# Start-up and last store of a one-core SiLU MLP forward and backward kernel: dummy matmuls, order and size of the first loads, buffers of the first transposes, and a split last group

## Chip, cores, metric

The kernel runs on one core of a Trainium2 chip. The metric is the device time of one execution in microseconds (us); lower is better. "Span" is the time from the first to the last instruction in a trace, which is about 2 us shorter than the device time. A run of a kernel is a set of executions; I quote medians and, where two kinds of execution appear, each kind. PE is the matmul engine (TensorE), DVE the vector engine, ACT the scalar engine, SP the engine that only issues transfers here.

## The reference

```python
B, S, D, F = 1, 2048, 640, 1536          # all bfloat16
def _fwd_reference(x, w1, w2):
    h = jnp.einsum("bsd,df->bsf", x, w1)
    h = silu(h)
    return jnp.einsum("bsf,fd->bsd", h, w2)
# results: out, and the gradients of x, w1, w2 for a given grad_out (jax.vjp)
```

## The kernel before

Work is cut into four chunks of 512 rows. Stage P of a chunk computes h = w1ᵀ·xᵀ and ga = w2·gᵀ for 12 tiles of F, five 512-wide matmuls each, and from them the activation and its gradient. Stage O multiplies back for out and the gradient of x. At the end come the two weight gradients, gw2 and gw1. The first chunk needs xᵀ, gᵀ and w2ᵀ, which PE makes by transposes into PSUM tiles (`tp` in the traces); DVE (0.49 us for 640 columns) or ACT (0.69 us) copies them to SBUF tiles (`xT_c`, `gT_c`, `w2T_sb`), from which PE's matmuls take them.

```python
    xn = gh_sb[:, NS - TPC : NS, 0:D]
    gn = a_sb[:, NS - TPC : NS, 0:D]
    nc.sync.dma_start(out=xn, in_=x2[0:SC, :]...)        # x, 640 KB, SP's queue
    nc.scalar.dma_start(out=gn, in_=g2[0:SC, :]...)      # grad_out, 640 KB, ACT's queue
    for fc in range(NFC):                                # three pieces of 512 columns or 4 row tiles
        nc.sync.dma_start(out=w1_sb[:, :, fc*FC:(fc+1)*FC], ...)       # 640 KB
        nc.scalar.dma_start(out=w2_sb[:, fc*FPC:(fc+1)*FPC, :], ...)   # 640 KB
    nc.sync.dma_start_transpose(out=w1T_sb[:], in_=w1[:, :])

    for t in range(TPC):                                 # 4 tiles of 128 rows
        tp = psO.tile([P, 16, P], bf16, tag="o")         # two buffers in all
        for i, src in enumerate((xn, gn)):
            for dk in range(ND):
                nc.tensor.transpose(tp[:, i*8 + dk, :], src[:, t, dk*P:(dk+1)*P], ident[:])
        nc.vector.tensor_copy(out=xT_c[...], in_=tp[:, 0:ND, :])
        nc.scalar.copy(out=gT_c[...], in_=tp[:, 8:8+ND, :])

    def w2T_transposes(fc): ...    # 20 transposes for 4 tiles; DVE copies 2048 wide, ACT 512 wide
    # ... stages P, T, O of four chunks, then gw2: not touched by the change
    groups = [(dt_, fc) for dt_ in range(ND) for fc in range(NFC)]     # gw1: 15 groups of 16 matmuls
    # ... pairs of groups; each is copied by ACT or DVE and stored; the 15th stands alone
```

Of the kernel before, what the change touches and what calls it, by code (L numbers as in the profile page):

```python
# [8 lines left out]
ACT = mybir.ActivationFunctionType  # L9
ALU = mybir.AluOpType  # L10
# [3 lines left out]
def kernel(  # L14
# [11 lines left out]
    nc = tc.nc  # L26
    P = 128
    bf16 = mybir.dt.bfloat16
    f32 = mybir.dt.float32
# [5 lines left out]
    NS, ND, NF = S // P, D // P, F // P  # L35
    FC = 512
    NFC = F // FC
    FPC = FC // P
    DH = D // 2
    SC = 512  # L40
    TPC = SC // P
    NCH = S // SC

    x2 = x.rearrange("b s d -> (b s) d")
    g2 = grad_out.rearrange("b s d -> (b s) d")
    o2 = out_0.rearrange("b s d -> (b s) d")
    gx2 = out_1.rearrange("b s d -> (b s) d")
    gw1 = out_2
# [4 lines left out]
    gh_sb = big.tile([P, NS, F], bf16)  # L53

    wO = ctx.enter_context(tc.tile_pool(name="wO", bufs=1))
    w2_sb = wO.tile([P, NF, D], bf16)
    w1T_sb = wO.tile([P, NF, D], bf16)
    ident = wO.tile([P, P], bf16)
# [6 lines left out]
    tmp = ctx.enter_context(tc.tile_pool(name="tmp", bufs=2))  # L65
    stage = ctx.enter_context(tc.tile_pool(name="stage", bufs=8))

    psO = ctx.enter_context(tc.tile_pool(name="psO", bufs=2, space=PSUM))
# [3 lines left out]
    psA = p1.enter_context(tc.tile_pool(name="psA", bufs=2, space=PSUM))  # L72

    w1_sb = early.tile([P, ND, F], bf16)
    w2T_sb = early.tile([P, ND, F], bf16)
    xT_c = early.tile([P, ND, SC], bf16)
    gT_c = early.tile([P, ND, SC], bf16)

    xn = gh_sb[:, NS - TPC : NS, 0:D]
    gn = a_sb[:, NS - TPC : NS, 0:D]  # L80
    nc.sync.dma_start(out=xn, in_=x2[0:SC, :].rearrange("(t p) d -> p t d", p=P))
    nc.scalar.dma_start(out=gn, in_=g2[0:SC, :].rearrange("(t p) d -> p t d", p=P))
    w1v = w1.rearrange("(k p) f -> p k f", p=P)
    w2v = w2.rearrange("(k p) d -> p k d", p=P)
    for fc in range(NFC):
        nc.sync.dma_start(
            out=w1_sb[:, :, fc * FC : (fc + 1) * FC], in_=w1v[:, :, fc * FC : (fc + 1) * FC]
        )
        nc.scalar.dma_start(
            out=w2_sb[:, fc * FPC : (fc + 1) * FPC, :], in_=w2v[:, fc * FPC : (fc + 1) * FPC, :]  # L90
        )
    nc.sync.dma_start_transpose(out=w1T_sb[:], in_=w1[:, :])

    for t in range(TPC):
        tp = psO.tile([P, 16, P], bf16, tag="o")
        for i, src in enumerate((xn, gn)):
            for dk in range(ND):
                nc.tensor.transpose(  # L98
                    tp[:, i * 8 + dk, :], src[:, t, dk * P : (dk + 1) * P], ident[:]
                )  # L100
        nc.vector.tensor_copy(out=xT_c[:, :, t * P : (t + 1) * P], in_=tp[:, 0:ND, :])  # L101
        nc.scalar.copy(out=gT_c[:, :, t * P : (t + 1) * P], in_=tp[:, 8 : 8 + ND, :])

    def w2T_transposes(fc):
        for dk0 in range(0, ND, 4):
            ndk = min(4, ND - dk0)
            tp = psO.tile([P, 16, P], bf16, tag="o")
            for i in range(ndk):
                for j in range(FPC):
                    ft = fc * FPC + j  # L110
                    nc.tensor.transpose(  # L111
                        tp[:, i * FPC + j, :],
                        w2_sb[:, ft, (dk0 + i) * P : (dk0 + i + 1) * P],
                        ident[:],
                    )
            src = tp[:, 0 : ndk * FPC, :].rearrange("p (i j) f -> p i (j f)", i=ndk)
            dst = w2T_sb[:, dk0 : dk0 + ndk, fc * FC : (fc + 1) * FC]
            if dk0 == 0:
                nc.vector.tensor_copy(out=dst, in_=src)  # L119
            else:  # L120
                nc.scalar.copy(out=dst, in_=src)

    def stage_P(c):
        for ft in range(NF):
            if c == 0 and ft % FPC == 0:
                w2T_transposes(ft // FPC)
            fsl = slice(ft * P, (ft + 1) * P)
            h_ps = psA.tile([P, SC], f32, tag="h")
            for dk in range(ND):
                nc.tensor.matmul(  # L130
                    h_ps[:], lhsT=w1_sb[:, dk, fsl], rhs=xT_c[:, dk, :],
                    start=(dk == 0), stop=(dk == ND - 1),
                )
            ga_ps = psA.tile([P, SC], f32, tag="ga")
            for dk in range(ND):
                nc.tensor.matmul(  # L136
                    ga_ps[:], lhsT=w2T_sb[:, dk, fsl], rhs=gT_c[:, dk, :],
                    start=(dk == 0), stop=(dk == ND - 1),
                )
            h3 = h_ps[:].rearrange("p (t s) -> p t s", t=TPC)  # L140
            ga3 = ga_ps[:].rearrange("p (t s) -> p t s", t=TPC)
            nc.scalar.activation(aT_c[:, :, ft, :], h3, ACT.Silu)  # L142
            nc.scalar.activation(h_ps[:], h_ps[:], ACT.Tanh, scale=0.5)  # L143
            omth = tmp.tile([P, TPC, P], f32, tag="omth")
            nc.scalar.activation(omth[:], h3, ACT.Identity, scale=-1.0, bias=1.0)  # L145
            nc.vector.scalar_tensor_tensor(  # L146
                out=omth[:], in0=aT_c[:, :, ft, :], scalar=-1.0, in1=omth[:],
                op0=ALU.add, op1=ALU.mult,
            )
            nc.vector.scalar_tensor_tensor(  # L150
                out=ghT_c[:, :, ft, :], in0=omth[:], scalar=2.0, in1=ga3,
                op0=ALU.add, op1=ALU.mult,
            )

    def stage_T(c):
        if c + 1 < NCH:
            nc.sync.dma_start_transpose(out=xT_c[:], in_=x2[(c + 1) * SC : (c + 2) * SC, :])
            nc.sync.dma_start_transpose(out=gT_c[:], in_=g2[(c + 1) * SC : (c + 2) * SC, :])
        for src, dst in ((aT_c, a_sb), (ghT_c, gh_sb)):
            nc.sync.dma_start_transpose(  # L160
                out=dst[:, c * TPC : (c + 1) * TPC, :].rearrange("p t (j r) -> p (t j) r", r=P),
                in_=src[:].rearrange("p t j s -> p (t j s)"),
            )
# [18 lines left out]

    for c in range(NCH):
        stage_P(c)
        if c == NCH - 1:
            p1.close()
            late = ctx.enter_context(tc.tile_pool(name="late", bufs=1))
            g_sb = late.tile([P, NS, D], bf16)
            x_sb = late.tile([P, NS, D], bf16)
            nc.sync.dma_start(out=g_sb[:], in_=g2.rearrange("(t p) d -> p t d", p=P))  # L190
            psW = ctx.enter_context(tc.tile_pool(name="psW", bufs=2, space=PSUM))
        stage_T(c)
        stage_O(c)
    nc.sync.dma_start(out=x_sb[:], in_=x2.rearrange("(t p) d -> p t d", p=P))

    for ft in range(NF):
        w_ps = psW.tile([P, 2, 512], f32, tag="w")
        for hf in range(2):
            for st in range(NS):
                nc.tensor.matmul(  # L200
                    w_ps[:, hf, :DH], lhsT=a_sb[:, st, ft * P : (ft + 1) * P],
                    rhs=g_sb[:, st, hf * DH : (hf + 1) * DH],
                    start=(st == 0), stop=(st == NS - 1),
                )
        w_sb = stage.tile([P, 2, DH], bf16, tag="o_sb")
        if ft % 2 == 0:
            nc.scalar.copy(out=w_sb[:], in_=w_ps[:, :, :DH])  # L207
        else:
            nc.vector.tensor_copy(out=w_sb[:], in_=w_ps[:, :, :DH])  # L209
        nc.sync.dma_start(  # L210
            out=gw2[ft * P : (ft + 1) * P, :], in_=w_sb[:].rearrange("p h d -> p (h d)")
        )
    groups = [(dt_, fc) for dt_ in range(ND) for fc in range(NFC)]
    for gi in range(0, len(groups), 2):
        pair = groups[gi : gi + 2]
        w_ps = psW.tile([P, 2, 512], f32, tag="w")
        for j, (dt_, fc) in enumerate(pair):
            for st in range(NS):
                nc.tensor.matmul(  # L219
                    w_ps[:, j, :], lhsT=x_sb[:, st, dt_ * P : (dt_ + 1) * P],  # L220
                    rhs=gh_sb[:, st, fc * FC : (fc + 1) * FC],
                    start=(st == 0), stop=(st == NS - 1),
                )
        for j, (dt_, fc) in enumerate(pair):
            w_sb = stage.tile([P, FC], bf16, tag="o_sb")
            if (gi + j) % 2 == 0:
                nc.scalar.activation(w_sb[:], w_ps[:, j, :], ACT.Copy, scale=0.5)  # L227
            else:
                nc.vector.tensor_scalar(  # L229
                    out=w_sb[:], in0=w_ps[:, j, :], scalar1=0.5, scalar2=None, op0=ALU.mult  # L230
                )
            nc.sync.dma_start(
                out=gw1[dt_ * P : (dt_ + 1) * P, fc * FC : (fc + 1) * FC], in_=w_sb[:]
            )


# [28 lines left out]
```

## Time and profile before

The median was 333.83 us (333.68 to 334.45, 5 executions). The profiled execution was a slowish one: 334.76 us, span 332.9 us.

Lines of the page of the kernel before: the span, PE's busy tenths in 40 slices of the span, and the shares by engine of the chain of work that ended last.

```profile
span 332.9 us, 4604 instructions
...
PE   1899999999999999999999999999999999999995
...
PE 92%; ACT 3%; DMA 2%; DVE 2%; issue 0%; ACTq 0%; DVEq 0%
```

PE is the bound, and only the two ends of the span have room. The waits of PE over the whole span (who waited for whom: us in total, times, longest) say how little there is in between.

```profile
PE tp L98 <- DMA gh_sb<-in_x_dram: 6.6, 1, 6.6
PE ga_ps L136 <- DVE w2T_sb L119: 0.6, 2, 0.3
PE h_ps L130 <- DVE xT_c L101: 0.6, 1, 0.6
PE tp L98 <- ACT gT_c L102: 0.2, 1, 0.2
```

PE waits 6.6 us for x, then little. But a busy PE need not be a fast one. The timeline of PE at the start (start us, duration us, engine, line, operation, names, count, idle time before) shows how fast it went.

```profile
6.63 0.71 PE L98 MATMUL tp<-ident,gh_sb 128*128 128x128 bf16 x5 [6.63 <-DMA gh_sb<-in_x_dram]
7.54 0.71 PE L98 MATMUL tp<-ident,a_sb 128*128 128x128 bf16 x5 [0.20 <-DMA a_sb<-in_grad_out_dram]
8.05 0.74 PE L98 MATMUL tp<-ident,gh_sb 128*128 128x128 bf16 x5
8.59 0.74 PE L98 MATMUL tp<-ident,a_sb 128*128 128x128 bf16 x5
9.56 0.69 PE L98 MATMUL tp<-ident,gh_sb 128*128 128x128 bf16 x5 [0.24 <-ACT gT_c L102]
...
12.44 0.59 PE L130 MATMUL h_ps<-xT_c,w_sb 128*128 128x512 bf16 x1 [0.58 <-DVE xT_c L101]
```

Five transposes start every 0.51 to 0.54 us, 107 ns apart. Of the twenty w2 transposes a little later, the first three (12.82, 12.93 and 13.03 us) are still 107 ns apart, and the rest 56 ns, by the start of each in the trace. PE ran at half rate until about 13.06 us, 6.4 us after the first of the transposes. Where the spacing halves like this I say below that the clock rose. (The profile's granted clock reads 1.00 through all of this, as its record in the trace begins only at 13.06 us. The spacing of the matmuls is what to read there.)

The transfers that PE needs first (names, queue, KB, median us from issue to landing):

```profile
w_sb<-in_w_dram ACTq DMA_DIRECT2D x3, 640.0 KB, 12.3
w_sb<-in_w_dram SPq DMA_DIRECT2D x3, 640.0 KB, 13.2
...
a_sb<-in_grad_out_dram ACTq DMA_DIRECT2D x1, 640.0 KB, 6.8
gh_sb<-in_x_dram SPq DMA_DIRECT2D x1, 640.0 KB, 5.8
```

And the end of the chain (start us, us, what): the last matmul ends at 329.41 us, the copy out of PSUM at 330.08, and 2.8 us more pass with the store and the end of the program.

```profile
321.03 8.38 PE w_ps L219 x38
...
329.48 0.60 ACT w_sb L227
```

### The profile page before, as it was taken

Reading aid. Unit: us, or ns where it says so; the run is one execution under the profiler, and the core shown is the slowest. Engines: PE = TensorE matmul, PEld = TensorE weight load, DVE = VectorE, ACT = ScalarE, POOL = GpSimd, SP = SyncE. Lnnn points to the kernel's source line nnn. Section 1 sums busy time; section 2 is a strip of 40 time slices with the busy share of each in tenths; the row PEclk is TensorE's granted clock in tenths of the full one; section 3 lists DMA queues with packets and bytes.
Section 4 is the critical chain, followed back from the end, with each engine's and each line's share of the span. In section 5 each row is a group of like instructions: output and inputs, shape, how many; then the busy total and the mean of one; then the engine's idle time right before and its main releaser. Section 6 shows DMA issues by size and latency. Waiting matters only on the chain.

```text
span 332.9 us, 4604 instructions
## 1 busy us (share of the span) xinstructions
PE 320.1 (96%) x1955; PEld 190.2 (57%) x1972; DVE 81.3 (24%) x116; ACT 123.5 (37%) x199; POOL 0.7 (0%) x6
## 2 busy tenths in 40 slices
PE   1899999999999999999999999999999999999995
PEld 1654467754467764457764447777777775444442
DVE  0366630016640006660005661000000000010000
ACT  1687732258851238862128882211000000010001
POOL 0000000000000000000000000000000000000000
PEclk9999999999999999999999999999999999999999
DMA  7990089920049950049990009999211001001101
GB/s 253 356 256 3 0 165 216 228 88 2 1 93 197 233 174 0 0 39 222 214 203 21 2 0 193 327 274 332 102 41 39 27 35 41 32 32 49 47 32 47
DMA packets 89923, 38.43 MB, mean 115 GB/s; under 512 B 73776, under 2 KB 89904, under 8 KB 89904
## 3 DMA queue, kind: packets, MB, share of 16 engines
q1 hardware_dynamic: 87792, 35.53, 46.7%
q10 hardware_dynamic: 2112, 2.62, 2.3%
q8 instruction: 15, 0.25, 0.3%
q14 instruction: 4, 0.03, 0.0%
HBM read 10.49 MB, written 9.18 MB: 59 GB/s over the span
## 4 chain that ended last, share of the span: by engine, by line
PE 92%; ACT 3%; DMA 2%; DVE 2%; issue 0%; ACTq 0%; DVEq 0%
PE o_ps L172 31%; PE w_ps L200 16%; PE w_ps L219 15%; PE ga_ps L136 14%; PE h_ps L130 14%; DMA a_sb<-in_grad_out_dram 2%; PE tp L98 1%; DVE w2T_sb L119 1%; DVE omth L146 1%; ACT omth L145 1%; ACT aT_c L142 1%; ACT h_ps L143 1%; ACT L142 0%; PE tp L111 0%; DVE xT_c L101 0%
## 5 line engine op out<-in xcount | busy, mean ns | idle before, releaser
L146 DVE SCALAR_TENSOR_TENSOR omth<-aT_c,omth 128x512 f32<-128x512 bf16 x48 | 33.3, 693 | 112.9 <-ACT omth L145 112.9
L136 PE MATMUL ga_ps<-gT_c,w2T_sb 128*128 128x512 bf16 x240 | 59.7, 379 | 0.8 <-DVE w2T_sb L119 0.6
L130 PE MATMUL h_ps<-xT_c,w_sb 128*128 128x512 bf16 x228 | 59.2, 380 | 1.2 <-DVE xT_c L101 0.6
L172 PE MATMUL o_ps<-w_sb,aT_c 128*128 128x320 bf16 x384 | 54.8, 299 | 0.0
L172 PE MATMUL o_ps<-w1T_sb,ghT_c 128*128 128x320 bf16 x384 | 54.8, 299 | 0.0
L178 ACT ACTIVATE o_sb<-o_ps 128x640 bf16<-128x640 f32 x32 | 22.5, 703 | 81.6 <-PE o_ps L172 81.6
L200 PE MATMUL w_ps<-g_sb,a_sb 128*128 128x320 bf16 x384 | 52.3, 299 | 0.0
L219 PE MATMUL w_ps<-gh_sb,x_sb 128*128 128x512 bf16 x235 | 51.7, 379 | 0.3
L172 PEld LDWEIGHTS <-aT_c 128*128 128x128 bf16 x384 | 37.5, 98 | 15.3
L200 PEld LDWEIGHTS <-a_sb 128*128 128x128 bf16 x384 | 37.5, 98 | 14.7
L172 PEld LDWEIGHTS <-ghT_c 128*128 128x128 bf16 x384 | 37.5, 98 | 14.7
L136 PEld LDWEIGHTS <-w2T_sb 128*128 128x128 bf16 x240 | 23.2, 98 | 29.9 <-DVE w2T_sb L119 1.9
L219 PEld LDWEIGHTS <-x_sb 128*128 128x128 bf16 x240 | 23.4, 98 | 28.2
L130 PEld LDWEIGHTS <-w_sb 128*128 128x128 bf16 x240 | 23.4, 98 | 27.1
L142 ACT ACTIVATE aT_c<-h_ps 128x512 bf16<-128x512 f32 x48 | 28.6, 597 | 16.0 <-PE h_ps L130 16.0
L150 DVE SCALAR_TENSOR_TENSOR ghT_c<-omth,ga_ps 128x512 bf16<-128x512 f32 x48 | 33.0, 687 | 5.2 <-DVE omth L146 0.5
L145 ACT ACTIVATE omth<-h_ps 128x512 f32<-128x512 f32 x48 | 28.7, 597 | 1.5
L143 ACT ACTIVATE h_ps<-h_ps 128x512 f32<-128x512 f32 x48 | 27.9, 582 | 1.5
L227 ACT ACTIVATE w_sb<-w_ps 128x512 bf16<-128x512 f32 x8 | 4.8, 597 | 51.3 <-PE w_ps L219 51.3
L209 DVE CAST w_sb<-w_ps 128x640 bf16<-128x640 f32 x6 | 4.9, 824 | 71.8 <-PE w_ps L200 71.8
L207 ACT CAST w_sb<-w_ps 128x640 bf16<-128x640 f32 x6 | 4.2, 692 | 43.7 <-PE w_ps L200 43.7
L229 DVE TENSOR_SCALAR w_sb<-w_ps 128x512 bf16<-128x512 f32 x7 | 4.8, 691 | 44.0 <-ACT w_sb L227 44.0
(18 smaller groups left out, 31.4 us busy)
## 6 DMA issues: line engine op xcount, KB each, us to landing
out_dram<-o_sb SPq DMA_DIRECT2D x32, 160.0 KB, 2.0
g_sb<-in_grad_out_dram SPq DMA_DIRECT2D x1, 2560.0 KB, 11.2
x_sb<-in_x_dram SPq DMA_DIRECT2D x1, 2560.0 KB, 10.9
w_sb<-in_w_dram ACTq DMA_DIRECT2D x3, 640.0 KB, 12.3
w_sb<-in_w_dram SPq DMA_DIRECT2D x3, 640.0 KB, 13.2
out_dram<-w_sb SPq DMA_DIRECT2D x12, 160.0 KB, 1.8
out_dram<-w_sb SPq DMA_DIRECT2D x15, 128.0 KB, 1.7
a_sb<-in_grad_out_dram ACTq DMA_DIRECT2D x1, 640.0 KB, 6.8
```

The lines of the kernel that those rows point to most:

```text
L130: nc.tensor.matmul(h_ps[:], lhsT=w1_sb[:, dk, fsl], rhs=xT_c[:, dk, :], start=(dk == 0), stop=(dk == ND - 1),)
L136: nc.tensor.matmul(ga_ps[:], lhsT=w2T_sb[:, dk, fsl], rhs=gT_c[:, dk, :], start=(dk == 0), stop=(dk == ND - 1),)
L142: nc.scalar.activation(aT_c[:, :, ft, :], h3, ACT.Silu)
L143: nc.scalar.activation(h_ps[:], h_ps[:], ACT.Tanh, scale=0.5)
L145: nc.scalar.activation(omth[:], h3, ACT.Identity, scale=-1.0, bias=1.0)
L146: nc.vector.scalar_tensor_tensor(out=omth[:], in0=aT_c[:, :, ft, :], scalar=-1.0, in1=omth[:], op0=ALU.add, op1=ALU.mult,)
L150: nc.vector.scalar_tensor_tensor(out=ghT_c[:, :, ft, :], in0=omth[:], scalar=2.0, in1=ga3, op0=ALU.add, op1=ALU.mult,)
L172: nc.tensor.matmul(o_ps[:, hf, :DH], lhsT=srcT[:, t, ft, :], rhs=wsb[:, ft, hf * DH : (hf + 1) * DH], start=(ft == 0), stop=(ft == NF - 1),)
L178: nc.scalar.activation(o_sb[:], o_ps[:, :, :DH], ACT.Copy, scale=scale)
L200: nc.tensor.matmul(w_ps[:, hf, :DH], lhsT=a_sb[:, st, ft * P : (ft + 1) * P], rhs=g_sb[:, st, hf * DH : (hf + 1) * DH], start=(st == 0), s ...
L209: nc.vector.tensor_copy(out=w_sb[:], in_=w_ps[:, :, :DH])
L219: nc.tensor.matmul(w_ps[:, j, :], lhsT=x_sb[:, st, dt_ * P : (dt_ + 1) * P], rhs=gh_sb[:, st, fc * FC : (fc + 1) * FC], start=(st == 0), s ...
```

## The change

The intent is to shorten both ends. (a) Nine dummy matmuls run while x is on its way, meant to have the clock up when x lands (in the kernel before it rose at 13.06 us), and an early Silu is to load ACT's table (in the kernel before the load took 1.28 us ahead of the first Silu, at 14.86 us). (b) x comes first, in halves on both queues, then grad_out. (c) w1 and w2 come in pieces of 1, 3, 4 and 4 tiles, and the w2 transposes in groups of 1, 3, 2, 2, 2, 2. (d) The first transposes use six PSUM buffers and both copy engines in turn, all of x before all of grad_out. (e) The last gw1 group of 512 columns is cut into 384 and 128; the last copy goes to DVE and the last store but one to ACT's queue. The function `keep_warm` in the changed kernel is never called.

```diff
+    warm = tmp.tile([P, SC], bf16, tag="omth")
+    nc.vector.memset(warm[:], 0.0)
+    warm_o = tmp.tile([P, 8], f32, tag="omth")
+    nc.scalar.activation(warm_o[:], warm[:, 0:8], ACT.Silu)
+    warm_ps = psO.tile([P, SC], f32, tag="o")
+    for i in range(N_WARM):                                  # N_WARM = 9
+        nc.tensor.matmul(warm_ps[:], lhsT=ident[:], rhs=warm[:], start=True, stop=True)
...
+    for dst, src in ((xn, x2), (gn, g2)):
+        for eng, t0 in ((nc.sync, 0), (nc.scalar, HT)):      # HT = 2 of the 4 tiles
+            eng.dma_start(out=dst[:, t0 : t0 + HT, :], in_=src[t0 * P : (t0 + HT) * P, :]...)
+    W_PIECES = ((0, 1), (1, 4), (4, 8), (8, 12))             # all on SP but the first piece of w2
+    for f0, f1 in W_PIECES:
+        for load in (load_w2, load_w1) if f0 == 1 else (load_w1, load_w2):
+            load(f0, f1)
...
+    for src, dstT, tag, eng in ((xn, xT_c, "h", "v"), (gn, gT_c, "ga", "s")):
+        for t in range(TPC):
+            tp = psA.tile([P, 8, P], bf16, tag=tag) if t < 2 else psO.tile([P, 8, P], bf16, tag="o")
+            ...                                              # 5 transposes
+            if (t % 2 == 0) == (eng == "v"): nc.vector.tensor_copy(...)
+            else: nc.scalar.copy(...)
...
+    W2T_GROUPS = {0: 1, 1: 3, 4: 2, 6: 2, 8: 2, 10: 2}       # even: copy on DVE, odd: on ACT
...
+    TAILW = 128
+    groups += [(dt_l, c0_l, c1_l - TAILW), (dt_l, c1_l - TAILW, c1_l)]   # both alone, the last on DVE
```

More of the change, by code (lines that the diff above doesn't have):

```diff
@@ L42 @@
     NCH = S // SC
+    N_WARM = 9
     x2 = x.rearrange("b s d -> (b s) d")
@@ L77 @@
     gT_c = early.tile([P, ND, SC], bf16)
+    warm = tmp.tile([P, SC], bf16, tag="omth")
[5 more added lines that the diff above has]
+        nc.tensor.matmul(warm_ps[:], lhsT=ident[:], rhs=warm[:], start=True, stop=True)
     xn = gh_sb[:, NS - TPC : NS, 0:D]
     gn = a_sb[:, NS - TPC : NS, 0:D]
-    nc.sync.dma_start(out=xn, in_=x2[0:SC, :].rearrange("(t p) d -> p t d", p=P))
@@ L82 @@
-    nc.scalar.dma_start(out=gn, in_=g2[0:SC, :].rearrange("(t p) d -> p t d", p=P))
     w1v = w1.rearrange("(k p) f -> p k f", p=P)
     w2v = w2.rearrange("(k p) d -> p k d", p=P)
-    for fc in range(NFC):
-        nc.sync.dma_start(
-            out=w1_sb[:, :, fc * FC : (fc + 1) * FC], in_=w1v[:, :, fc * FC : (fc + 1) * FC]
-        )
-        nc.scalar.dma_start(
-            out=w2_sb[:, fc * FPC : (fc + 1) * FPC, :], in_=w2v[:, fc * FPC : (fc + 1) * FPC, :]
-        )
-    nc.sync.dma_start_transpose(out=w1T_sb[:], in_=w1[:, :])
@@ L94, with load_w1, load_w2 @@
-    for t in range(TPC):
+    HT = TPC // 2
+    for dst, src in ((xn, x2), (gn, g2)):
+        for eng, t0 in ((nc.sync, 0), (nc.scalar, HT)):
+            eng.dma_start(
+                out=dst[:, t0 : t0 + HT, :],
+                in_=src[t0 * P : (t0 + HT) * P, :].rearrange("(t p) d -> p t d", p=P),
+            )
+    W_PIECES = ((0, 1), (1, 4), (4, 8), (8, 12))
+    def load_w1(f0, f1):
+        nc.sync.dma_start(out=w1_sb[:, :, f0 * P : f1 * P], in_=w1v[:, :, f0 * P : f1 * P])
+    def load_w2(f0, f1):
+        eng = nc.scalar if f0 == 0 else nc.sync
+        eng.dma_start(out=w2_sb[:, f0:f1, :], in_=w2v[:, f0:f1, :])
@@ new lines, with keep_warm @@
+    for f0, f1 in W_PIECES:
+        for load in (load_w2, load_w1) if f0 == 1 else (load_w1, load_w2):
+            load(f0, f1)
+    nc.sync.dma_start_transpose(out=w1T_sb[:], in_=w1[:, :])
+    def keep_warm(n):
+        for _ in range(n):
+            nc.tensor.matmul(warm_ps[:], lhsT=ident[:], rhs=warm[:], start=True, stop=True)
+    for src, dstT, tag, eng in ((xn, xT_c, "h", "v"), (gn, gT_c, "ga", "s")):
+        for t in range(TPC):
+            if t < 2:
+                tp = psA.tile([P, 8, P], bf16, tag=tag)
+            else:
+                tp = psO.tile([P, 8, P], bf16, tag="o")
+            for dk in range(ND):
+                nc.tensor.transpose(tp[:, dk, :], src[:, t, dk * P : (dk + 1) * P], ident[:])
+            if (t % 2 == 0) == (eng == "v"):
+                nc.vector.tensor_copy(out=dstT[:, :, t * P : (t + 1) * P], in_=tp[:, 0:ND, :])
+            else:
+                nc.scalar.copy(out=dstT[:, :, t * P : (t + 1) * P], in_=tp[:, 0:ND, :])
@@ L95, with w2T_transposes @@
+    def w2T_transposes(ft0, n):
         tp = psO.tile([P, 16, P], bf16, tag="o")
-        for i, src in enumerate((xn, gn)):
-            for dk in range(ND):
+        for dk in range(ND):
+            for j in range(n):
                 nc.tensor.transpose(
-                    tp[:, i * 8 + dk, :], src[:, t, dk * P : (dk + 1) * P], ident[:]
+                    tp[:, dk * n + j, :], w2_sb[:, ft0 + j, dk * P : (dk + 1) * P], ident[:]
                 )
-        nc.vector.tensor_copy(out=xT_c[:, :, t * P : (t + 1) * P], in_=tp[:, 0:ND, :])
@@ L102 @@
-        nc.scalar.copy(out=gT_c[:, :, t * P : (t + 1) * P], in_=tp[:, 8 : 8 + ND, :])
-    def w2T_transposes(fc):
-        for dk0 in range(0, ND, 4):
-            ndk = min(4, ND - dk0)
-            tp = psO.tile([P, 16, P], bf16, tag="o")
-            for i in range(ndk):
-                for j in range(FPC):
-                    ft = fc * FPC + j
-                    nc.tensor.transpose(
-                        tp[:, i * FPC + j, :],
-                        w2_sb[:, ft, (dk0 + i) * P : (dk0 + i + 1) * P],
-                        ident[:],
-                    )
-            src = tp[:, 0 : ndk * FPC, :].rearrange("p (i j) f -> p i (j f)", i=ndk)
-            dst = w2T_sb[:, dk0 : dk0 + ndk, fc * FC : (fc + 1) * FC]
-            if dk0 == 0:
-                nc.vector.tensor_copy(out=dst, in_=src)
-            else:
-                nc.scalar.copy(out=dst, in_=src)
+        src = tp[:, 0 : n * ND, :].rearrange("p (i j) f -> p i (j f)", i=ND)
@@ L123, in stage_P @@
+        dst = w2T_sb[:, :, ft0 * P : (ft0 + n) * P]
+        if ft0 % 2 == 0:
+            nc.vector.tensor_copy(out=dst, in_=src)
+        else:
+            nc.scalar.copy(out=dst, in_=src)
+    W2T_GROUPS = {0: 1, 1: 3, 4: 2, 6: 2, 8: 2, 10: 2}
     def stage_P(c):
         for ft in range(NF):
-            if c == 0 and ft % FPC == 0:
-                w2T_transposes(ft // FPC)
+            if c == 0 and ft in (0, 1):
+                w2T_transposes(ft, W2T_GROUPS[ft])
+            if c == 0 and ft >= 3 and ft + 1 in W2T_GROUPS:
+                w2T_transposes(ft + 1, W2T_GROUPS[ft + 1])
@@ L212 @@
         )
-    groups = [(dt_, fc) for dt_ in range(ND) for fc in range(NFC)]
-    for gi in range(0, len(groups), 2):
-        pair = groups[gi : gi + 2]
+    groups = [(dt_, fc * FC, (fc + 1) * FC) for dt_ in range(ND) for fc in range(NFC)]
+    dt_l, c0_l, c1_l = groups.pop()
+    TAILW = 128
+    groups += [(dt_l, c0_l, c1_l - TAILW), (dt_l, c1_l - TAILW, c1_l)]
+    n_g = len(groups)
+    for gi in list(range(0, n_g - 2, 2)) + [n_g - 2, n_g - 1]:
+        pair = groups[gi : gi + 2] if gi < n_g - 2 else groups[gi : gi + 1]
         w_ps = psW.tile([P, 2, 512], f32, tag="w")
-        for j, (dt_, fc) in enumerate(pair):
+        for j, (dt_, c0, c1) in enumerate(pair):
             for st in range(NS):
                 nc.tensor.matmul(
-                    w_ps[:, j, :], lhsT=x_sb[:, st, dt_ * P : (dt_ + 1) * P],
-                    rhs=gh_sb[:, st, fc * FC : (fc + 1) * FC],
+                    w_ps[:, j, : c1 - c0], lhsT=x_sb[:, st, dt_ * P : (dt_ + 1) * P],
+                    rhs=gh_sb[:, st, c0:c1],
                     start=(st == 0), stop=(st == NS - 1),
                 )
-        for j, (dt_, fc) in enumerate(pair):
+        for j, (dt_, c0, c1) in enumerate(pair):
             w_sb = stage.tile([P, FC], bf16, tag="o_sb")
-            if (gi + j) % 2 == 0:
-                nc.scalar.activation(w_sb[:], w_ps[:, j, :], ACT.Copy, scale=0.5)
+            last = gi + j == len(groups) - 1
+            if (gi + j) % 2 == 0 and not last:
+                nc.scalar.activation(w_sb[:, : c1 - c0], w_ps[:, j, : c1 - c0], ACT.Copy, scale=0.5)
             else:
                 nc.vector.tensor_scalar(
-                    out=w_sb[:], in0=w_ps[:, j, :], scalar1=0.5, scalar2=None, op0=ALU.mult
-                )
-            nc.sync.dma_start(
-                out=gw1[dt_ * P : (dt_ + 1) * P, fc * FC : (fc + 1) * FC], in_=w_sb[:]
-            )
+                    out=w_sb[:, : c1 - c0], in0=w_ps[:, j, : c1 - c0], scalar1=0.5, scalar2=None,
+                    op0=ALU.mult,
+                )
+            eng = nc.scalar if (gi + j) == len(groups) - 2 else nc.sync
+            eng.dma_start(out=gw1[dt_ * P : (dt_ + 1) * P, c0:c1], in_=w_sb[:, : c1 - c0])
 _INS = ['x', 'w1', 'w2', 'grad_out']
```

## The prediction

> **What bounds the kernel now.** TensorE: PE is 96% busy on the page and 92% of the chain of waits. Between the first transpose (6.63 us) and the last matmul's end (329.41 us) it hardly stops. In the timeline 512-wide matmuls are spaced 216 ns, 320-wide ones 136 ns, so matmuls alone need 720 x 0.216 + 1152 x 0.136 = 312 us. About 21 us of the 332.9 us span is something else:
> - head: 6.6 us waiting for x (waits of PE);
> - 40 transposes of x and grad_out, 6.63 to 12.4 us, spaced 107 ns; the w2 transposes at 12.82 us are spaced about 60 ns, so PE ran at half rate until then;
> - 60 w2 transposes, 3.6 us;
> - stalls in the first P stage, 1.3 us: the second activation table load (1.28 us at 14.86) delays Silu and stalls ga 0.3 us, and 1.22 us w2T copies hold ga back 0.3 us twice;
> - tail: 3.5 us after the last matmul (eviction 0.60 us, store about 1.7 us, end).
>
> From 43.4 us to the last group the change touches nothing.
>
> **What the change does.**
> 1. Nine dummy matmuls from about 1.4 us: 9 x 0.427 (estimate, twice 0.216) = 3.8 us, ending near 5.3 us. [...] Real transposes should run at about 60 ns: 40 take 2.5 us instead of 4.3 us.
> 2. x split over both queues ahead of grad_out. The fine windows show data from 2.5 us at 330 to 400 GB/s, now shared by x and grad_out (landing 6.6 and 7.5). I expect x at 5.2 to 6.2 us, grad_out at about 7.
> 3. Transposes in six PSUM buffers, copies split between DVE (0.49 us) and ACT (0.69 us): PE no longer waits for copies.
> 4. Weights in pieces, w2 transposes in groups: the first real matmul needs only a small piece of w1.
> 5. Silu table loaded early: saves the 0.3 us stall.
> 6. New cost: the second group (1920 wide) is copied by ACT, about 1.8 us (estimate from 0.58 for 512, 0.69 for 640), behind tile 0's Silu, tanh and identity; ga of tile 1 should stall about 0.75 us.
> 7. Tail: last group cut into 384 + 128. PE +0.2 us, last eviction about 0.3 instead of 0.6 us, store about as long. Net -0.1 to -0.3 us.
>
> **On the critical path.** All of the head is, as PE is dense afterwards. Transposes end near 8.2 us, first h matmul near 9 us instead of 12.44. The first P stage then takes 29.3 + 0.75 us, ending near 39.1 instead of 43.3: -4.1. With the tail -4.2 us, 1.3%; even a perfect head would barely give 2%.
>
> **Prediction:** 329.6 us, 8 in 10 between 328.4 and 331.4. Faster by over 2%: 0.04; within 2%: 0.95; slower: 0.01.
>
> **What would show it.** First real transpose at 5.3 to 6 us, spaced about 60 ns; first h matmul 8.5 to 9.5 us; one table load; first o_ps matmul near 39; the stretch from there to the last w_ps group unchanged within 0.3 us; span ending about 3.2 us after the last matmul.
>
> **What would make it wrong.** The clock released only during the transposes (+1.7 us). The early Silu delaying ACT's queue, so half of x comes 1.3 us late. [...] The ACT copy stalling more than one tile.

-4.1 us at the head and -0.1 us at the tail make -4.2 us, from 333.83 to 329.6 us. That nine dummies would have the clock up when x lands was my estimate; the trace of the kernel before showed only the rise 6.4 us after its first transposes.

## The result and the profile after

The changed kernel took 328.56 us (328.38 to 329.28, 8 executions) against 334.29 us (15). The ratio is 0.9832, 95% interval 0.9818 to 0.9846. The ratio is that of the mean times (8 executions over 15), so not quite the ratio of the medians quoted. It is 1.7% or 5.6 us: within 2%, inside the range, and 1.4 us more than the 4.2 us that the prediction expected.

The same lines of the page, for the changed kernel:

```profile
span 326.4 us, 4662 instructions
...
PE   7999999999999999999999999999999999999996
...
PE 96%; DMA 2%; issue 0%; SPq 0%; DVE 0%
```

All waits of PE in the changed kernel:

```profile
PE warm_ps L86 <- POOL ident masks.py:199: 1.4, 1, 1.4
PE h_ps L154 <- DMA w_sb<-in_w_dram: 0.4, 1, 0.4
```

The timeline of PE at the start:

```profile
1.35 4.02 PE L86 MATMUL warm_ps<-warm,ident 128*128 128x512 bf16 x9 [1.35 <-POOL ident masks.py:199]
5.17 1.40 PE L123 MATMUL tp<-ident,gh_sb 128*128 128x128 bf16 x20
6.41 1.42 PE L123 MATMUL tp<-ident,a_sb 128*128 128x128 bf16 x20
8.22 0.59 PE L154 MATMUL h_ps<-xT_c,w_sb 128*128 128x512 bf16 x2 [0.40 <-DMA w_sb<-in_w_dram]
```

Twenty transposes now start within 1.24 us (6.41 - 5.17), 62 ns apart in the mean: the first three are still 107 ns apart, as the clock rose only at 5.41 us in this execution, and the others 56 ns. The first h matmul comes at 8.22 instead of 12.44 us, and it waits for nothing but its weights. The transfers:

```profile
gh_sb<-in_x_dram ACTq DMA_DIRECT2D x1, 320.0 KB, 4.2
gh_sb<-in_x_dram SPq DMA_DIRECT2D x1, 320.0 KB, 3.9
...
w_sb<-in_w_dram SPq DMA_DIRECT2D x1, 160.0 KB, 6.2
```

And the end of the chain. The last matmul ends at 323.64 us, the last copy at 323.95, the span 2.45 us later.

```profile
315.22 8.42 PE w_ps L247 x54
...
323.66 0.29 DVE w_sb L258
```

Where the time went, from the two traces: the first o_ps matmul of stage O starts at 37.44 instead of 43.26 us (-5.8); from there to the end of the last matmul it is 286.20 instead of 286.15 us (unchanged); from there to the end of the span 2.8 instead of 3.5 us (-0.7). That is 6.5 us of span, more than the 5.7 us between the median times, for two reasons. The profiled execution of before was slow: the 11 executions of before beside the first experiments had a median span of 332.3 us. And device time minus span was about 1.9 us for before and 2.2 us for the changed kernel. What those 0.3 us outside the span are is open; kernels without dummy matmuls showed 1.8 to 1.9, those with them mostly 2.0 to 2.2.

### The profile page after: what moved, and what is told of

It reads as the page before. It is cut to its first block, busy times and chain, and to the rows that moved or that the text cites. A ratio compares the mean times of both kernels' runs of the same rounds, so it can differ in the third digit from the quotient of the medians. Undisturbed runs are those within 1.5% of the kernel's fastest.

```text
span 326.4 us, 4662 instructions
## 1 busy us (share of the span) xinstructions
PE 321.0 (98%) x1979; PEld 190.9 (59%) x1997; DVE 81.6 (25%) x120; ACT 122.1 (37%) x197; POOL 0.7 (0%) x6
## 4 chain that ended last, share of the span: by engine, by line
PE 96%; DMA 2%; issue 0%; SPq 0%; DVE 0%
PE o_ps L196 32%; PE w_ps L224 16%; PE ga_ps L160 16%; PE w_ps L247 16%; PE h_ps L154 16%; DMA w_sb<-in_w_dram 2%; PE tp L133 1%; SPq L95 0%; DVE w_sb L258 0%
## 5 line engine op out<-in xcount | busy, mean ns | idle before, releaser
L247 PE MATMUL w_ps<-gh_sb,x_sb 128*128 128x512 bf16 (+2 forms) x251 | 51.7, 365 | 0.3
L247 PEld LDWEIGHTS <-x_sb 128*128 128x128 bf16 x256 | 24.5, 98 | 27.5
L256 ACT ACTIVATE w_sb<-w_ps 128x512 bf16<-128x512 f32 (+1 forms) x8 | 4.7, 584 | 50.4 <-PE w_ps L247 50.4
L258 DVE TENSOR_SCALAR w_sb<-w_ps 128x512 bf16<-128x512 f32 (+1 forms) x8 | 5.1, 642 | 46.2 <-ACT w_sb L256 44.0
```

Source lines behind the costliest of these rows:

```text
L247: nc.tensor.matmul(w_ps[:, j, : c1 - c0], lhsT=x_sb[:, st, dt_ * P : (dt_ + 1) * P], rhs=gh_sb[:, st, c0:c1], start=(st == 0), stop=(st == ...
L258: nc.vector.tensor_scalar(out=w_sb[:, : c1 - c0], in0=w_ps[:, j, : c1 - c0], scalar1=0.5, scalar2=None, op0=ALU.mult,)
```

## The experiments

Each ran correctly, with rounds that let a few tenths of a microsecond be seen. The kernel before, run beside them, had medians of 334.20, 334.30 and 334.35 us, so I compare medians with the changed kernel's 328.56 us and call differences below 0.3 us small. In the runs of the changed kernel with one part undone, the order of PE's other work is the same, except where I say so. No run undid the new grouping of the w2 transposes alone (the second half of (c)), so its share is not known: PE's matmuls waited 0.6 us for copies of w2T in the kernel before and not at all in the changed one.

### Undo the dummy matmuls

```diff
-    N_WARM = 9
+    N_WARM = 0
```

> The changed kernel without its nine dummy matmuls; the order of all other PE work is the same. Theory A (clock and arrival share the head): transposes start as x lands (about 5.0 us) but are spaced 107 ns, the clock is released about 6 us later, first h matmul near 9.4 instead of 8.22 us and the next few matmuls cold; 1.7 us slower than the changed kernel (1.2 to 2.0). Rival B (the clock is nearly all of it): over 4 us slower, close to before. Rival C (the loads are all of it): under 0.5 us slower, as PE would wait for weights anyway.

It took 328.78 us (328.52 to 329.22, 4 executions): 0.2 us slower, against my 1.7. The timeline of PE shows why:

```profile
4.62 2.31 PE L123 MATMUL tp<-ident,gh_sb 128*128 128x128 bf16 x20 [4.62 <-DMA gh_sb<-in_x_dram]
6.73 1.95 PE L123 MATMUL tp<-ident,a_sb 128*128 128x128 bf16 x20
8.51 0.38 PE L154 MATMUL h_ps<-xT_c,w_sb 128*128 128x512 bf16 x1
```

The transposes are indeed slow at first. But they start 0.55 us earlier (the dummies had held PE until 5.17, while x was there at 4.62), they run without a gap, and the clock rises by itself near 8.12 us, 3.5 us after the first of them (the starts in the trace are 107 ns apart until then, and 56 ns from there on). By 8.51 us PE is at the first h matmul, only 0.3 us later than with dummies, because with dummies PE stood 0.4 us waiting for the first weights. Faster transposes mostly bought a longer wait. The time is the one that rival C named, but its reason, that the loads are all of it, does not hold: other parts, below, count too.

### The dummy matmuls alone, on the kernel before

```diff
+    warm = tmp.tile([P, SC], bf16, tag="omth")
+    nc.vector.memset(warm[:], 0.0)
+    warm_ps = psO.tile([P, SC], f32, tag="o")
+    for i in range(9):
+        nc.tensor.matmul(warm_ps[:], lhsT=ident[:], rhs=warm[:], start=True, stop=True)
```

> The kernel before with nothing but the nine dummy matmuls added. Theory A: transposes at about 60 ns spacing from 6.6 us, then PE waits for the first 512-wide pieces of w1 and w2, which land near 10.8 us; first h matmul near 10.9 instead of 12.44 us; 1.7 us faster than before (1.3 to 2.2). Rival B: over 4 us faster. Rival C: no gain.

It took 334.80 us (334.01 to 335.18): no gain at all, against the 1.7 us that I expected. In the timeline there are nine dummies, then a pause of 1.01 us ahead of x, and the transposes are 107 ns apart again (from 7.28 to the next group of five at 7.79).

```profile
6.39 0.71 PE L104 MATMUL tp<-ident,gh_sb 128*128 128x128 bf16 x5 [1.01 <-DMA gh_sb<-in_x_dram]
7.28 0.71 PE L104 MATMUL tp<-ident,a_sb 128*128 128x128 bf16 x5 [0.17 <-DMA a_sb<-in_grad_out_dram]
7.79 0.74 PE L104 MATMUL tp<-ident,gh_sb 128*128 128x128 bf16 x5
```

### Twelve dummy matmuls on the kernel before

```diff
-    for i in range(9):
+    for i in range(12):
```

> The kernel before with twelve dummy matmuls in place of nine, so that they end (1.35 + 12 x 0.427 = 6.5 us) as x lands and PE never pauses ahead of the transposes. Theory G (nine gave nothing there because the one-microsecond pause ahead of x let the clock stay low or fall back): transposes spaced 60 ns, then a wait for the first weights until about 10.9 us; 1.5 us faster than before (0.8 to 2), with a run or two slower where the wait for weights lowers the clock again. Rival H (weights and copies hold PE whatever its clock): within 0.4 us of before.

It took 333.12 us (332.95 to 333.23): 1.2 us faster than before, within what was expected. The pause ahead of x is down to 0.43 us, and the transposes are fast (five in 0.28 us):

```profile
7.54 0.45 PE L104 MATMUL tp<-ident,a_sb 128*128 128x128 bf16 x5 [0.44 <-DMA a_sb<-in_grad_out_dram]
7.82 0.44 PE L104 MATMUL tp<-ident,gh_sb 128*128 128x128 bf16 x5
...
9.29 0.44 PE L104 MATMUL tp<-ident,gh_sb 128*128 128x128 bf16 x5 [0.75 <-ACT gT_c L108]
```

The last line shows the next limit: PE waits 0.75 us for ACT's copy to free a PSUM buffer. In the kernel before that wait was 0.24 us, since slow transposes had hidden it. The wait for weights until about 10.9 us that I expected did not come: the first h matmul starts at 11.19 us, after 0.58 us of waiting for the last copy of x.

### Undo the loads: order and pieces as before

```diff
-    (x and grad_out in halves on both queues; W_PIECES)
+    nc.sync.dma_start(out=xn, ...)
+    nc.scalar.dma_start(out=gn, ...)
+    for fc in range(NFC): (w1 on SP, w2 on ACT, three pieces each, as before)
```

> The changed kernel with the loads of before (x on one queue, grad_out on the other, weights in 512-wide pieces on two queues); the PE order is the same as in the changed kernel. Theory A: first transpose at 6.6 us, transposes done near 8.9, then PE waits for the first weight pieces until about 10.8 us; 2.3 us slower than the changed kernel (1.8 to 2.8). Rival B: under 0.7 us slower. Rival C: over 4 us slower.

The median is 331.60 us, with two kinds of execution: four at 331.42 to 331.73 with a mean granted clock of 1.000, and two at 333.05 with 0.995. The first kind is 2.9 us slower than the changed kernel, just outside the 1.8 to 2.8 expected. In the profile, which fell on the second kind, PE waits until 10.93 us for weights; the clock is at half from 10.92 to 14.33 us.

```profile
6.42 1.29 PE L114 MATMUL tp<-ident,gh_sb 128*128 128x128 bf16 x20 [1.62 <-DMA gh_sb<-in_x_dram]
10.93 1.46 PE L145 MATMUL h_ps<-xT_c,w_sb 128*128 128x512 bf16 x3 [1.96 <-DMA w_sb<-in_w_dram]
```

The pause of 1.62 us behind the dummies did no harm here: in this execution the dummies' spacing falls from 427 to 217 ns at 4.1 us, so the clock was up before the pause, and the transposes are fast.

### Undo the weight pieces alone

```diff
-    W_PIECES = ((0, 1), (1, 4), (4, 8), (8, 12)) and its loop
+    for fc in range(NFC): (w1 on SP, w2 on ACT, three pieces each, as before)
```

> The changed kernel keeps x ahead of grad_out, in halves on both queues, but takes w1 and w2 in the three large pieces of before; the PE order is the same. Theory P (the small first weight pieces are what counts): 1.64 MB lies ahead of PE in one case, 2.62 MB in the other, so the first h matmul waits until about 10.9 us as with all the old loads; 2.7 us slower than the changed kernel (2.2 to 3.2), some runs more if PE's pause costs it the clock. Rival X (x first is what counts): under 1 us slower.

The median is 332.71 us: two executions at 331.19 and 331.40 (clock 1.000), four at 332.69 to 332.78 (0.995). The first kind is the same as with all loads undone: x ahead of grad_out, in halves on two queues, brings nothing while the first real matmul needs a 640 KB piece of w1, issued beside as much of w2 on the other queue. The transfers of all queues together moved 353 to 371 GB/s in each microsecond from 5 to 11 us here, at a DMA share of 1.07 to 1.09, and 353 to 360 GB/s at 1.08 to 1.10 from 6 to 12 us in the kernel before. PE's wait:

```profile
PE h_ps L150 <- DMA w_sb<-in_w_dram: 3.4, 1, 3.4
```

What the pause does to the clock, in windows of the profiled execution, of the slower kind (the window; its length; busy us and instructions of PE, PEld, DVE, ACT, POOL; then granted clock, DMA share, GB/s):

```profile
11.40:11.50 0.10, 0.10 (x4) 0.10 (x3) 0.00 (x0) 0.00 (x0) 0.00 (x0) 0.79 1.06 346
11.50:11.60 0.10, 0.10 (x5) 0.10 (x3) 0.00 (x0) 0.00 (x0) 0.00 (x0) 0.50 1.08 356
...
14.80:14.90 0.10, 0.10 (x2) 0.10 (x1) 0.10 (x1) 0.00 (x0) 0.00 (x0) 0.65 1.06 348
```

A clock of 0.79 means that it fell 0.42 of the way into that window (1 - 0.5 x 0.42), at 11.46 us; 0.65 puts the rise at 14.87. The half rate lasted 3.4 us. PE already worked again from 10.94 us: the penalty came after the pause, as in the run with all loads undone, where PE worked again from 10.93 us and the clock was at half from 10.92 to 14.33 us, also 3.4 us. In this trace the clock's record begins with its first rise at 4.63 us, where the dummies' spacing falls from 427 to 216 ns, 6.83 us ahead of the fall; in the run with all loads undone the two are 4.09 and 10.92 us, again 6.83 apart. What sets these times is not shown.

### The same with dummies in the pause

```diff
+    keep_ps = psA.tile([P, SC], f32, tag="h")
+    for _ in range(14):
+        nc.tensor.matmul(keep_ps[:], lhsT=ident[:], rhs=xT_c[:, 0, :], start=True, stop=True)
```

> The changed kernel with the large weight pieces of before (as in the run with old weight pieces) and fourteen dummy matmuls (3.0 us at 0.216) in the 3.4 us in which PE waits there for weights. Theory W (the pause costs the clock; 4 of 6 executions without the dummies took 332.7 and showed a mean clock of 0.995, the other 2 took 331.3 at 1.0): all executions near 331.3 at mean clock 1.0. Rival V (the slower executions come from late weights): both kinds still there.

It took 331.41 us (330.93 to 331.75, 4 executions), all at a mean clock of 1.000. The slower kind is gone although the weights come no earlier (the first h matmul starts at 10.86 us, against 10.94), so the pause was its cause. (PE's order differs a little: five transposes of w2 stand ahead of the first h matmul here, and four stand behind the first ga instead of ahead of it.) With the clock held, large pieces cost 2.8 us against small ones.

### Undo x first alone

```diff
-    for dst, src in ((xn, x2), (gn, g2)): (halves on both queues)
+    nc.sync.dma_start(out=xn, ...)
+    nc.scalar.dma_start(out=gn, ...)
```

> The changed kernel with x whole on one queue and grad_out whole on the other, as before, but with the new small weight pieces; the PE order is the same. Theory P: x lands near 6.4 and grad_out near 7.3 us, transposes done near 9.0, first h matmul near 9.1 instead of 8.2 us; 0.9 us slower than the changed kernel (0.5 to 1.4). Rival X: 2 us slower or more.

Two kinds again: 329.49 and 329.82 us, and four from 330.93 to 331.16. The profile, of the slower kind, shows a pause of 1.14 us between the dummies and x, then transposes at 107 ns until 10.34 us, 3.8 us after the first:

```profile
6.52 2.31 PE L118 MATMUL tp<-ident,gh_sb 128*128 128x128 bf16 x20 [1.14 <-DMA gh_sb<-in_x_dram]
8.62 2.10 PE L118 MATMUL tp<-ident,a_sb 128*128 128x128 bf16 x20
```

### The same with twelve dummies

```diff
-    N_WARM = 9
+    N_WARM = 12
```

> The changed kernel with x and grad_out whole on one queue each, and twelve dummy matmuls in place of nine, so that no pause lies ahead of the first transpose (with nine it was 1.1 us, and 4 of 6 executions took 331.0 with cold transposes, 2 of 6 329.6). Theory W: all executions near 329.6, transposes spaced 60 ns. Rival V: still two kinds, 329.6 and 331.0.

All four executions took 329.52 to 329.61 us, as theory W said, and the transposes are fast:

```profile
6.45 1.29 PE L118 MATMUL tp<-ident,gh_sb 128*128 128x128 bf16 x20
7.58 1.42 PE L118 MATMUL tp<-ident,a_sb 128*128 128x128 bf16 x20
```

So x first is worth 1.0 us by itself, and it also closes the pause behind nine dummies, which was worth 1.4 us more in most executions. Twelve dummies both close the pause and last longer, and this run does not separate the two. The run of twelve on the kernel before, where a pause of 0.43 us was left and the clock had risen at 5.6 us, during the dummies, speaks for the second: there the clock was up before PE paused, and the transposes stayed fast (five in 0.28 us).

### Undo the transposes' buffers, order and copies

```diff
-    for src, dstT, tag, eng in ((xn, xT_c, "h", "v"), (gn, gT_c, "ga", "s")): ...
+    for t in range(TPC):
+        tp = psO.tile([P, 16, P], bf16, tag="o")      # x and grad_out together, two buffers
+        ...                                           # x copied by DVE, grad_out by ACT
```

> The changed kernel with the transposes of before: x and grad_out tile by tile in two shared PSUM buffers, all x copies on DVE, all grad_out copies on ACT. The second x tile now waits in PE's order for grad_out, and the third pair waits for ACT's 0.69 us copy of the first: transposes end near 8.7, first h matmul near 8.9 instead of 8.2 us; 0.7 us slower than the changed kernel (0.4 to 1.2). Rival: no difference, as PE waits for the weights until 8.2 us anyway.

It took 330.35 us (330.29 to 330.45): 1.8 us slower, more than twice my estimate. Buffers, order and copies were undone together, so their shares are not known. (Four w2 transposes also stand behind the first ga instead of ahead of it.) The two largest waits of PE in the first 12 us behind the dummies; a third, for grad_out, took 0.3 us:

```profile
PE tp L120 <- ACT gT_c L124: 0.7, 1, 0.7
PE h_ps L151 <- DVE xT_c L123: 0.6, 1, 0.6
```

The transposes end near 9.4 us, and the first h matmul then waits 0.58 us for the copy of the last x tile, which this order makes last; I had left that out. It starts at 9.98 us, 1.76 us after the changed kernel's 8.22, and the time agrees.

### Undo the split of the last group

```diff
-    groups += [(dt_l, c0_l, c1_l - TAILW), (dt_l, c1_l - TAILW, c1_l)]
+    (15 whole groups, as before)
```

> The changed kernel with the last gw1 group whole, as before. From the two traces (end of span minus end of last matmul 3.5 us before, 2.8 us after, PE work equal within 0.1 us): 0.65 us slower than the changed kernel. The prediction on record had put this at 0.1 to 0.3 us. If the tail is worth nothing, the same time and all the gain lies in the head.

It took 328.81 us (328.78 to 328.97): 0.25 us slower, within the 0.1 to 0.3 us rather than the 0.65 us that I read from the two spans. In its trace the copy ends 0.67 us after the last matmul, in the changed kernel's 0.31 us; that is 0.36 us. The store of the last 32 KB took 1.4 us from issue to landing, that of 128 KB 1.7 us. Why the times differ by less than these two together is open; executions of the changed kernel alone spread over 0.9 us, so 0.25 us is barely resolved.

### Undo the early Silu

```diff
-    warm_o = tmp.tile([P, 8], f32, tag="omth")
-    nc.scalar.activation(warm_o[:], warm[:, 0:8], ACT.Silu)
```

> The changed kernel without the early Silu, so that the table for Silu is loaded after the last copy of grad_out, as before. Prediction on record: the early load is worth 0.3 us. From the changed kernel's trace: ACT runs Silu, tanh, identity and the 1.76 us copy of w2T back to back from 9.56 us, and ga of tile 1 waits for that copy; a load of 1.28 us ahead of Silu delays the copy by up to 1.1 us (it could begin 0.2 us early), and PE has no other work queued ahead of ga; 0.9 us slower than the changed kernel (0.5 to 1.2).

It took 328.67 us (328.56 to 328.81): 0.1 us, not resolved, against my 0.9. ACT had nothing to do from 8.76 us until the first h tile was complete, so most of the table load fits into that time:

```profile
8.78 1.28 ACT L164 ACT_TABLE_LOAD   x1
...
10.07 0.60 ACT L164 ACTIVATE aT_c<-h_ps 128x512 bf16<-128x512 f32 x1
```

Silu starts 0.5 us later than in the changed kernel (9.56 us), and ga of tile 1 only 0.2 us later (13.62 against 13.40).

### Move the 1920-wide copy of w2T to DVE

```diff
-        if ft0 % 2 == 0:
+        if True:                     # always nc.vector.tensor_copy
```

> The changed kernel with the 1920-wide copy of w2T moved from ACT to DVE. In the changed kernel's trace this copy takes 1.76 us on ACT, starts at 11.59 us, and ga of tile 1 waits 0.40 us for it; by DVE's times (1.22 us for 2048) it would take about 1.15 us, start at the same time, and end 0.6 us earlier. 0.2 to 0.4 us faster than the changed kernel if that wait is on the chain; no difference if DVE's own work ahead of it takes up the gain. Would beat both kernels if it holds.

It took 329.05 us (328.67 to 329.46, 4 executions): not faster than the changed kernel. The copy is shorter (1.15 us, against 1.76 on ACT), but DVE, busy with tile 0's gradient from 12.11 us, starts it only at 12.72, where ACT had started at 11.59:

```profile
12.72 1.15 DVE L139 COPY w2T_sb<-tp 128x1920 bf16<-128x1920 bf16 x1
...
13.93 1.25 PE L160 MATMUL ga_ps<-gT_c,w2T_sb 128*128 128x512 bf16 x5 [0.19 <-DVE w2T_sb L139]
```

Two more things changed in this execution. Seven h matmuls instead of nine stand ahead of that ga in PE's order, so less work covers the copy. And the x transposes ran at half rate, as the clock rose only at 7.07 us:

```profile
5.17 2.19 PE L123 MATMUL tp<-ident,gh_sb 128*128 128x128 bf16 x20
```

So what the shorter copy alone gains is open. No kernel that ran beat the changed one.

## Why the prediction was right, and where its steps were off

**The bound and the total.** PE bound the kernel and the change touched only the two ends: right, with the 286.2 us between the first o_ps matmul and the last matmul unchanged within 0.05 us. The time was inside the range. The gain was undersized by 1.4 us, about 0.5 us of which is the kernel before itself, slower beside the changed kernel (334.29 us) than in the five executions that the prediction started from (333.83 us). Of the signs, the spacing, the one table load and the unchanged stretch came; the first transpose (5.17 us), the first h matmul (8.22), the first o_ps matmul (37.44) and the end (2.8 us after the last matmul) all came earlier than stated. The parts were weighed wrongly: the largest gain that was given microseconds, the faster transposes (1.8 us), is worth 0.2 us by itself, and the two worth most had been given none of their own. That their sum still came near was in part luck.

What each part is worth, as the loss when it alone is undone (with the clock held where two kinds appear):

| part undone | us lost | prediction or later estimate |
|---|---|---|
| small weight pieces (dummies in the pause) | 2.8 | 2.7, estimated after the result |
| buffers, order and copies of the transposes | 1.8 | 0.7, estimated after the result |
| x first (twelve dummies) | 1.0 | 0.9, estimated after the result |
| dummy matmuls | 0.2 | 1.8 for the transposes |
| split of the last group | 0.25 | 0.1 to 0.3 |
| early Silu | 0.1 | 0.3 |

The last three lie within the 0.9 us over which the changed kernel's own executions spread, and are not resolved by time alone. The sum is 6.2 us against the 5.7 us gained. It need not agree: undoing one part can uncover a wait that another had hidden, the grouping of the w2 transposes is not in the table, and each line is good to a few tenths.

1. **"40 take 2.5 us instead of 4.3 us."** They do, 62 ns apart. But the step treated this as time on the chain. With dummies PE waits for weights until 8.22 us, and without them the clock rose by itself 3.5 us into gapless transposes, so PE was only 0.3 us late at the first h matmul. It is the term that was most wrong: 1.8 us, 0.2 measured.
2. **"I expect x at 5.2 to 6.2 us."** Its first half landed at about 4.6 us and both by 5.0 us (issue at 0.73 plus 3.9 and 4.2). So the transposes ended early enough for the first h matmul to come at 8.22 instead of "near 9" us, which is one source of the extra gain. What set the 8.22 was the first piece of w1 (issue at 1.75 plus 6.2 us), for which PE waited 0.40 us. The early Silu did not delay ACT's transfers: they were issued at 0.73 and 1.31 us, before and during the table load (1.25 us).
3. **"PE no longer waits for copies."** Right, and worth 1.8 us together with the order, where the profile before showed such waits of only 0.24 us among the transposes and 0.58 us ahead of the first h matmul. A slow PE hid the rest: with fast transposes the 0.24 us became 0.75.
4. **"The first real matmul needs only a small piece of w1."** Right, and the largest part.
5. **The early Silu, 0.3 us.** 0.1 us, not resolved.
6. **"ga of tile 1 should stall about 0.75 us."** The copy took 1.76 us as estimated, but the weight load for ga waited only 0.40 us, and PE itself showed no gap: nine h matmuls, four of them of tile 2, stand ahead of that ga in PE's order. The P stage from the first h matmul to the first o_ps matmul took 29.2 us (37.44 - 8.22) instead of 30.05. This is the other source of the extra gain.
7. **The tail, -0.1 to -0.3 us.** 0.25 us.

**Of the warnings,** the first (clock up late) is real. Behind a pause it cost 1.4 us in most executions (331.0 against 329.6 us, 4 of 6 with x first undone). Without a pause it is common but cheap: x's transposes begin between 4.8 and 5.2 us, and of the seven profiles with x first behind nine dummies, four show the clock rise after that (5.41 us in the changed kernel, 5.90 without the early Silu, 6.50 with the old buffers, 7.07 with the copy on DVE) and three before it (4.35, 4.63, 4.89). The first h matmul came at 8.22, 8.15 and 8.42 us with the rise at 5.41, 5.90 and 7.07, and at 7.92 with the rise at 4.89. The changed kernel's times lie within 0.9 us of each other and show no second kind; whether a late clock makes their spread was not seen. With the small pieces the rate of the transfers was lower, 308 GB/s in the microsecond from 6 us against 370 in the run with the old weight pieces, and not enough to matter; why it was lower is not shown.

**What stays open:** the 0.3 us outside the span, and why some executions behind a pause keep their clock and others do not. The first rise lies anywhere from 2.7 to 5.7 us after the first dummy (where no pause of about 1 us came before it). Of the three runs with two kinds of execution, the profile shows the slower kind alone, so what differed in the others is not shown.

## What to carry to other kernels

At the start of a kernel, order the loads by when PE needs them and make the first piece of each small: small pieces were worth 2.8 us here and x first 1.0; beside these, more buffers with another order and other copies of the transposes were worth 1.8 us, and a warmer clock 0.2. Dummy matmuls helped here where the clock was up before PE paused, and without a pause of about 1 us it rose 2.7 to 5.7 us after the first of them: nine (4.02 us in the traces) with a pause of 1.01 or 1.14 us behind them gained nothing in most executions, and twelve (4.85 and 5.07 us) did their work in all ten, by the times. A later pause could still cost the clock: after 1.96 us without work it fell in 2 of 6 executions (all loads undone) and after 3.4 us in 4 of 6 (weight pieces undone), for 3.4 us in both traces. Where real work could start without gaps soon enough, it raised the clock nearly as well: without dummies the clock rose 3.5 us after the first transpose, and the time was 0.2 us longer. A wait that looks small in a profile taken at half clock can be the next limit once PE runs at full rate, as 0.24 us became 0.75 here, so cost it from the copies' durations, not from the wait.
